# Attention's elementwise work moved from Pool to ACT and DVE, and k's halves copied by DVE instead of DMA

## The chip, the cores and the metric

The kernel runs on one core of a Trainium2 chip. The metric is the device time of one execution in microseconds. A core has five engines with queues of their own: PE (matrix products), DVE (vector work), ACT (activations and scaled copies), Pool (general work) and SP, which here only issues DMA transfers. DMA transfers run on 16 engines that the core shares among its queues.

## The reference

Three stages follow one another. The arrays are float32.

```python
# attention: B, H, S, D = 8, 8, 576, 64, causal in blocks of 64
scores = (1 / sqrt(D)) * q @ k.T, masked to block_i >= block_j
attn = softmax(scores);  x = (attn @ v) as [4608, 512]
# gated MoE without routing: w1, w2 [512, 1024], w3 [1024, 1024], w_out [1024, 512]
x = ((x @ w1) * (x @ w2)) @ w3 @ w_out
# routed experts: 8 experts, 576 tokens each, assigned greedily by sorted logits x @ w_gate
out[tokens of e] = relu(x[tokens of e] @ ew1[e]) @ ew2[e]
```

## The kernel before

**Split numbers.** To multiply float32 data on PE in f16, a tensor is scaled by a power of two and split into hi, its f16 rounding, and lo, the f16 rounding of what is left. A product is hi*hi + hi*lo + lo*hi. The power of two comes from a sum of squares: `ssq` on ACT (L115), `total` on PE (L453), `pow2` on DVE (L75 to L78).

**The steps of attention.** A step n (0 to 31) handles one pair of heads of one batch, and `step(n)` (L648) writes its work in order. `s_tiles` (L217) computes the scores of nine query blocks i = 0 to 8 in six tiles: S on PE (L226), the row maximum on DVE (L231, with L284 for row 8), exp on ACT (L265, L286, L287), the sum and its reciprocal on DVE (L289, L237, L238). `fin` (L241) then writes the hi and lo of the probabilities into `Pb`: hi of row blocks 4 to 7 on Pool (L250), of 8 on DVE (L254), of 0 to 3 on ACT (L252), and lo on DVE (L255). Row block i is (i+1) x 64 wide; `blocks` (L205) cuts it into a first piece of up to 384 columns and pieces of at most 128. `transP` (L306) sends `Pb` through two DMA transposes, and `pv` (L312) of the next step multiplies by v.

**Preparation for later steps.** Between the first tile and the others, step n loads q and k of step n+2 (`load_qk`), prepares q and k of step n+1 (`prep_qk`, L175) and the part of v it needs (`prep_v`, L147). `prep_qk` scales on Pool in place (L193), rounds to hi on ACT (L194), subtracts to lo on Pool (L195); step 0 alone does this on ACT and DVE (L189, L190). A DMA transpose on SP's queue (L197) then gives `T`: T[:, 0] has q with hi in partitions 0 to 63 and lo in 64 to 127, T[:, 1] has k likewise, and T[:, 2] is to have k's halves exchanged. Two transfers on SP's queue (L200) copy the halves crosswise. `qkT` has two buffers, `qk16` one. The second transfer of step 0 is `gate["d"]`: the loads of v of the first batch are issued behind it (L607).

**Weights.** Spread over the steps through `fills`, w1, w2 and w3 are decoded on DVE (`decode`, L429) and split by `scaled` (L443): Pool, ACT, Pool. `wo_split` (L494) does the split on ACT and DVE already. From step 5 on, `moe_unit` (L341) computes the first matmuls of the MoE in between (L356, L361, L363), four units a step.

**Order.** Each engine runs its instructions in the order in which a planner put them, from a model of their durations; SP issues its transfers in order too, and a transfer whose data are not there holds the queue. An instruction waits for those of other engines by semaphores. After attention comes the rest of the MoE, then the routing, then the experts; Pool works there too (L966, L1103, L1150), and the diff doesn't touch that.

## Time and profile before

| | |
|---|---|
| runs shown | 1695.24, 1699.73, 1700.19 us; median 1699.73 |
| profiled execution | 1691.84 us, its span 1690.1 us |
| mean granted clock of PE | 0.941 |
| busy share of the span | PE 84%, DVE 67%, ACT 51%, Pool 30% |
| DVE's busy time up to 880 us, by the four stretches 0, 40, 360 and 400 us on | 14.60 + 295.12 + 22.70 + 387.24 us |

The shares are means over stages that have different limits, so the profile is read by stretches: 0 to about 880 us is attention with the first MoE matmuls, to about 960 us the rest of those, to about 1300 us the routing beside the last product, and then the experts. A busy time of an engine counts the time in which at least one of its instructions runs; an instruction that stands inside for something else counts as busy too. "Idle before" is the time that an engine stood still ahead of an instruction, and the name behind the arrow is what ended it.

### The profile page before, as it was taken

Reading aid. Unit: us, or ns where it says so; the run is one execution under the profiler, and the core shown is the slowest. Engines: PE = TensorE matmul, PEld = TensorE weight load, DVE = VectorE, ACT = ScalarE, POOL = GpSimd, SP = SyncE. Lnnn points to the kernel's source line nnn. Section 1 sums busy time; section 2 is a strip of 40 time slices with the busy share of each in tenths; the row PEclk is TensorE's granted clock in tenths of the full one; section 3 lists DMA queues with packets and bytes.
Section 4 is the critical chain, followed back from the end, with each engine's and each line's share of the span. In section 5 each row is a group of like instructions: output and inputs, shape, how many; then the busy total and the mean of one; then the engine's idle time right before and its main releaser. Section 6 shows DMA issues by size and latency. Waiting matters only on the chain.

```text
span 1690.1 us, 32656 instructions
## 1 busy us (share of the span) xinstructions
PE 1414.7 (84%) x11561; PEld 944.3 (56%) x11561; DVE 1136.9 (67%) x3972; ACT 863.1 (51%) x2211; POOL 500.2 (30%) x629
## 2 busy tenths in 40 slices
PE   1547768878788988889999988888886999999997
PEld 0325545556455655556566666655655656666664
DVE  3999999767897988888632178898884324353420
ACT  4666667656676666666432224343431456573721
POOL 4555654334654545454311000000002321100101
PEclk9867989989899999999999999999997999999999
DMA  7697988987999999997997352432435765462200
GB/s 170 131 189 163 195 195 198 194 187 154 188 188 211 182 208 194 192 205 160 241 233 242 103 194 77 143 130 90 144 101 134 197 133 180 132 191 84 82 26 31
DMA packets 575476, 270.04 MB, mean 160 GB/s; under 512 B 467281, under 2 KB 544593, under 8 KB 575313
## 3 DMA queue, kind: packets, MB, share of 16 engines
q1 hardware_dynamic: 567872, 246.95, 62.9%
q0 software_dynamic: 5760, 18.90, 3.5%
q10 hardware_dynamic: 1680, 2.11, 0.4%
q8 instruction: 90, 1.47, 0.3%
q14 instruction: 74, 0.60, 0.1%
HBM read 131.57 MB, written 39.86 MB: 101 GB/s over the span
## 4 chain that ended last, share of the span: by engine, by line
PE 26%; DVE 20%; issue 14%; DMA 8%; ACT 4%; POOL 2%; SPq 2%; POOLq 0%; ACTq 0%; DVEq 0%
PE px L976 7%; PE ab L356 6%; PE pe L1128 4%; DVE P L255 3%; PE pe L1145 3%; DVE gl L993 2%; DVE junk L231 2%; DMA qkT<-qk 2%; DMA xg<-xr,idx 1%; POOL out_dram L1150 1%; PE lgp L397 1%; ACT gh L991 1%; DVE row L1006 1%; PE PV L552 1%; DVE ewb L1057 1%
## 5 line engine op out<-in xcount | busy, mean ns | idle before, releaser
L356 PE MATMUL ab<-xT,w2h 128*128 128x288 f16 x1536 | 229.7, 299 | 23.5 <-DVE g L363 22.9
L255 DVE SCALAR_TENSOR_TENSOR P<-E,rr,P 128x64 f16<-128x64 f32 (+3 forms) x480 | 239.4, 534 | 11.4 <-POOL P L250 7.9
L356 PE MATMUL ab<-xT,w1h 128*128 128x288 f16 x1536 | 232.0, 300 | 18.0 <-DVE xT L336 7.9
L1128 PE MATMUL pe<-xT,ewa 128*128 128x288 f16 (+2 forms) x1728 | 193.8, 276 | 11.2 <-DMA xT<-xg 10.3
L356 PEld LDWEIGHTS <-w2h 128*128 128x128 f16 x1536 | 150.2, 102 | 84.8 <-issue 40.7
L356 PEld LDWEIGHTS <-w1h 128*128 128x128 f16 x1536 | 150.6, 103 | 77.6 <-issue 33.2
L250 POOL TENSOR_SCALAR P<-E,rr 128x384 f16<-128x384 f32 (+3 forms) x224 | 117.7, 537 | 250.6 <-DVE rr L238 122.6
L265 ACT ACTIVATE E<-S,nb,cc 128x256 f32<-128x256 f32 (+7 forms) x256 | 149.2, 587 | 81.7 <-DVE junk L231 47.5
L1145 PE MATMUL pe<-ewb,h 128*128 128x512 f16 (+1 forms) x960 | 189.1, 379 | 1.1 <-DVE h L1131 1.1
L226 PE MATMUL S<-qkT 128*64 128x64 f16 (+7 forms) x1280 | 132.1, 323 | 63.4 <-DMA qkT<-qkT 21.1
L1128 PEld LDWEIGHTS <-ewa 128*128 128x128 f16 x1728 | 158.4, 100 | 45.4 <-issue 11.8
L1103 POOL DMA_INDIRECT xg<-xr,idx x36 | 34.8, 965 | 481.7 <-DVE idx L952 387.9
L231 DVE TENSOR_SCALAR_CACHE_REDUCE junk<-S,cc 128x512 f16<-128x512 f32 (+4 forms) x320 | 155.1, 508 | 16.8 <-PE S L226 16.6
L1145 PEld LDWEIGHTS <-h 128*128 128x128 f16 (+1 forms) x960 | 85.4, 101 | 100.4 <-issue 3.8
L1131 DVE SCALAR_TENSOR_TENSOR h<-pe,h 128x288 f16<-128x288 f32 (+2 forms) x144 | 57.6, 420 | 109.0 <-ACT h L1130 106.5
L226 PEld LDWEIGHTS <-qkT 128*64 128x64 f16 x1280 | 65.8, 119 | 110.8 <-issue 67.7
L329 PE MATMUL PV<-PT,v 128*64 128x256 f16 (+4 forms) x1536 | 105.0, 264 | 25.2 <-DMA PT<-P 20.4
L976 PE MATMUL px<-W34l,gh 128*128 128x512 f32 x288 | 122.7, 426 | 0.0
L976 PE MATMUL px<-W34h,gh 128*128 128x512 f32 x288 | 122.0, 424 | 0.0
L976 PE MATMUL px<-W34h,gl 128*128 128x512 f32 x288 | 121.7, 423 | 0.0
L363 DVE SCALAR_TENSOR_TENSOR g<-ab,vr,a_sb 128x288 f32<-128x288 f32 x124 | 63.1, 508 | 76.9 <-PE ab L356 39.9
L329 PEld LDWEIGHTS <-v 128*64 128x64 f16 (+1 forms) x1536 | 75.9, 113 | 61.1 <-issue 55.8
(283 smaller groups left out, 2539.5 us busy)
## 6 DMA issues: line engine op xcount, KB each, us to landing
g<-gd SPq DMA_DIRECT2D x36, 512.0 KB
gd<-g SPq DMA_DIRECT2D x124, 144.0 KB
g<-gd SPq DMA_DIRECT2D x15, 1152.0 KB
raw<-in_moe_w_dram SPq DMA_DIRECT2D x32, 512.0 KB
esa<-in_moe_w_dram SPq DMA_DIRECT2D x8, 2048.0 KB
esb<-in_moe_w_dram SPq DMA_DIRECT2D x8, 2048.0 KB
xr<-row SPq DMA_DIRECT2D x36, 256.5 KB
qkT<-qkT SPq DMA_DIRECT2D x64, 144.0 KB
```

What stands on the lines that cost most here:

```text
L226: nc.tensor.matmul(ps[hh * 64:hh * 64 + 64, o:o + N], T[:, 0, qc:qc + 64], T[:, z, kc:kc + N], start=z == 1, stop=z == 2)
L231: nc.vector.tensor_scalar(j[:, :N], ps[:, o:o + N], c[:, 1:2], None, op0=ALU.mult, op1=ALU.min, accum_out=dst)
L250: nc.gpsimd.tensor_scalar(hi, src, r, 1.0, op0=ALU.mult, op1=ALU.mult)
L255: nc.vector.scalar_tensor_tensor(lo, src, r, hi, op0=ALU.mult, op1=ALU.subtract)
L265: nc.scalar.activation(e[:, o:o + N], ps[:, o:o + N], AF.Exp, bias=nb[:, 0, x:x + 1], scale=c[:, 0:1], accum_out=nb[:, 1, x:x + 1])
L329: nc.tensor.matmul(ps[hh * 64:hh * 64 + 64, (lo - i0) * 64:(i1 - i0) * 64], vt[:kk, zv, hh, j, :], t[:kk, zp, ix:ix + i1 - lo, hh * 64:hh ...
L356: nc.tensor.matmul(p[:, :288], w[:, zw, cc, :], x[:, zx, cc, c0:c0 + 288], start=first, stop=cc == 3 and zw == 1)
L363: nc.vector.scalar_tensor_tensor(g, ps["w2"][:, :288], iv[b][:, 1, f:f + 1], a, op0=ALU.mult, op1=ALU.mult)
L976: nc.tensor.matmul(p, gh[a][:, f], W34[b][:, f], start=f == 0 and a + b == 0, stop=f == 7 and a == 1)
L1128: nc.tensor.matmul(p[:, :n], w1[:, a, cc, f * P:(f + 1) * P], t[:, 4 * b + cc, x], start=cc == 0 and a + b == 0, stop=cc == 3 and a == 1)
L1131: nc.vector.scalar_tensor_tensor(h[:, 1, f, x], p[:, :n], 0.0, h[:, 0, f, x], op0=ALU.max, op1=ALU.subtract)
L1145: nc.tensor.matmul(p[r0:r1], h[:, a, f, k_ * P + r0:k_ * P + r1], EW[e, "b"][0][:, b, f], start=f == 0 and a + b == 0, stop=f == 7 and a == 1)
```

## The change

A new function `split` writes hi on ACT with the scale and lo on DVE from the unscaled data and the scale. `prep_v`, `prep_qk`, `scaled` and `wo_split` use it, so that nothing elementwise is left on Pool in this stage. In `fin`, hi of row blocks 5, 7 and 8 is on DVE and of the others on ACT. The crosswise copies of k's halves are instructions of DVE, and `gate["d"]` is now the transpose.

```diff
--- before.py
+++ after.py
@@ -29,8 +29,7 @@
 R3 = 2
 LE = 37
 SW = 30
-POOL_HI = (4, 5, 6, 7)
-DVE_HI = (8,)
+DVE_HI = (5, 7, 8)
 TH = 5
 TB = 15
 TBX = 5
@@ -98,6 +97,10 @@
     ps_s = pa.enter_context(tc.tile_pool(name="ps_s", bufs=3, space=PSUM))
     ps_v = pa.enter_context(tc.tile_pool(name="ps_v", bufs=2, space=PSUM))
 
+    def split(hi, lo, x, s):
+        nc.scalar.activation(hi, x, AF.Copy, scale=s)
+        nc.vector.scalar_tensor_tensor(lo, x, s, hi, op0=ALU.mult, op1=ALU.subtract)
+
     gate = {}
     qk32, qkT, vst, vhl, xT, PT = {}, {}, {}, {}, {}, {}
     sc_c, iv, sv, ivs = {}, {}, {}, {}
@@ -152,9 +155,7 @@
         h = slice(2 * hp, 2 * hp + 2)
         for a, z in ((t[:, h, :4, :], lambda y: vt[:, y, :, :4, :]), (t[:64, h, 4, :], lambda y: vt[:64, y, :, 4, :])):
             np_ = a.shape[0]
-            nc.gpsimd.tensor_scalar(a, a, s[:np_], 1.0, op0=ALU.mult, op1=ALU.mult)
-            nc.scalar.activation(z(0), a, AF.Copy)
-            nc.gpsimd.tensor_tensor(out=z(1), in0=a, in1=z(0), op=ALU.subtract)
+            split(z(0), z(1), a, s[:np_])
         vhl[n] = vt
 
     def scale_x(b):
@@ -185,19 +186,12 @@
         sc_c[n] = c
         t16 = c2.tile([P, 2, 9, 2, D], F16, name="qk16", bufs=1)
         for z in range(2):
-            if n == 0:
-                nc.scalar.activation(t16[:, z, :, 0, :], t[:, z], AF.Copy, scale=s[:, z:z + 1])
-                nc.vector.scalar_tensor_tensor(t16[:, z, :, 1, :], t[:, z], s[:, z:z + 1], t16[:, z, :, 0, :],
-                                               op0=ALU.mult, op1=ALU.subtract)
-                continue
-            nc.gpsimd.tensor_scalar(t[:, z], t[:, z], s[:, z:z + 1], 1.0, op0=ALU.mult, op1=ALU.mult)
-            nc.scalar.activation(t16[:, z, :, 0, :], t[:, z], AF.Copy)
-            nc.gpsimd.tensor_tensor(out=t16[:, z, :, 1, :], in0=t[:, z], in1=t16[:, z, :, 0, :], op=ALU.subtract)
+            split(t16[:, z, :, 0, :], t16[:, z, :, 1, :], t[:, z], s[:, z:z + 1])
         T = c2.tile([P, 3, 9 * P], F16, name="qkT")
-        nc.sync.dma_start_transpose(out=T[:, :2].rearrange("p z (c r) -> p (z c) r", r=P),
-                                    in_=t16.rearrange("p z c h d -> p (z c h d)"))
+        d = nc.sync.dma_start_transpose(out=T[:, :2].rearrange("p z (c r) -> p (z c) r", r=P),
+                                        in_=t16.rearrange("p z c h d -> p (z c h d)"))
         for x in range(2):
-            d = nc.sync.dma_start(T[64 * (1 - x):64 * (2 - x), 2], T[64 * x:64 * x + 64, 1])
+            nc.vector.tensor_copy(T[64 * (1 - x):64 * (2 - x), 2], T[64 * x:64 * x + 64, 1])
         qkT[n] = T
         if n == 0:
             gate["d"] = d
@@ -246,12 +240,10 @@
                     src = e[:, k0:k0 + n_].rearrange("p (b c) -> p b c", c=P)
                 else:
                     hi, lo, src = pb[:, 0, idx, :n_], pb[:, 1, idx, :n_], e[:, k0:k0 + n_]
-                if i in POOL_HI:
-                    nc.gpsimd.tensor_scalar(hi, src, r, 1.0, op0=ALU.mult, op1=ALU.mult)
-                elif i not in DVE_HI:
+                if i in DVE_HI:
+                    nc.vector.tensor_scalar(hi, src, r, None, op0=ALU.mult)
+                else:
                     nc.scalar.activation(hi, src, AF.Copy, scale=r)
-                else:
-                    nc.vector.tensor_scalar(hi, src, r, None, op0=ALU.mult)
                 nc.vector.scalar_tensor_tensor(lo, src, r, hi, op0=ALU.mult, op1=ALU.subtract)
 
         def some(ps, lst):
@@ -442,9 +434,7 @@
 
     def scaled(w, m2, hi, lo, name):
         s, e = pow2(sm, m2, name)
-        nc.gpsimd.tensor_scalar(w, w, s, 1.0, op0=ALU.mult, op1=ALU.mult)
-        nc.scalar.activation(hi, w, AF.Copy)
-        nc.gpsimd.tensor_tensor(out=lo, in0=w, in1=hi, op=ALU.subtract)
+        split(hi, lo, w, s)
         return e
 
     def total(m):
@@ -500,8 +490,7 @@
         t = wo["t"] = stg.tile([P, 8, 2, 512], F16, name="wo16", bufs=1)
         for c in range(8):
             w = wo["w"][:, c]
-            nc.scalar.activation(t[:, c, 0], w, AF.Copy, scale=s)
-            nc.vector.scalar_tensor_tensor(t[:, c, 1], w, s, t[:, c, 0], op0=ALU.mult, op1=ALU.subtract)
+            split(t[:, c, 0], t[:, c, 1], w, s)
         wo["wg"], wo["eg"] = hilo(wo["g"], 4, "wgx")
 
     def wo_dot():
```

## Rows read from the trace of the kernel before

**Rows 1.** Busy us (instructions) of each engine by stretch, from the view of stretches
```profile
core 0: us, PE busy (x) PEld busy (x) DVE busy (x) ACT busy (x) POOL busy (x), PEclk, DMA share, GB/s
40.00:360.00 320.00, 221.37 (x1914) 148.84 (x1914) 295.12 (x995) 210.06 (x591) 170.15 (x218) 0.84 0.87 182
400.00:880.00 480.00, 418.10 (x3837) 272.39 (x3836) 387.24 (x1305) 286.75 (x794) 222.01 (x296) 0.95 0.94 198
880.00:960.00 80.00, 77.98 (x609) 52.35 (x609) 15.74 (x38) 21.55 (x41) 9.33 (x4) 0.98 0.65 203
```

**Rows 2.** The chain that ended last, 400 to 880 us, shares by line
```profile
by line: DVE P L255 11.5%; PE ab L356 10.8%; DVE junk L231 6.9%; issue 6.5%; DMA qkT<-qk 5.6%; PE PV L552 3.6%; PE PV L329 3.3%; DMA PT<-P 2.7%; DVE g L363 2.7%; DVE nb L289 2.5%; DVE rr L237 2.4%; PE S L226 1.9%; ACT E L286 1.8%; DVE P L25
```

**Rows 3.** DVE's groups by shape, 0 to 880 us (count | busy us, mean ns | idle before)
```profile
L255 DVE SCALAR_TENSOR_TENSOR P<-E,rr,P 128x384 f16<-128x384 f32 x128 | 91.1, 712 | 6.8 <-POOL P L250 6.7
L255 DVE SCALAR_TENSOR_TENSOR P<-E,rr,P 128x64 f16<-128x64 f32 x160 | 61.7, 396 | 1.8 <-ACT P L252 1.7
L255 DVE SCALAR_TENSOR_TENSOR P<-E,rr,P 128x128 f16<-128x128 f32 x128 | 58.7, 460 | 1.0 <-ACT P L252 0.8
L289 DVE TENSOR_TENSOR nb<-nb 128x1 f32<-128x1 f32 x32 | 22.3, 696 | 23.8 <-ACT E L287 23.8
```

**Rows 4.** The same groups from 840.5 to 850.4 us, and that stretch's engines
```profile
840.50:850.40 9.90, 9.90 (x70) 5.12 (x69) 7.76 (x33) 4.73 (x13) 0.00 (x0) 0.78 0.94 163
L255 DVE SCALAR_TENSOR_TENSOR P<-E,rr,P 128x384 f16<-128x384 f32 x2 | 1.2, 612 | 0.0
L255 DVE SCALAR_TENSOR_TENSOR P<-E,rr,P 128x64 f16<-128x64 f32 x3 | 0.8, 276 | 0.0
L255 DVE SCALAR_TENSOR_TENSOR P<-E,rr,P 128x128 f16<-128x128 f32 x1 | 0.3, 344 | 0.0
L289 DVE TENSOR_TENSOR nb<-nb 128x1 f32<-128x1 f32 x1 | 0.2, 159 | 0.9 <-ACT E L287 0.9
L254 DVE TENSOR_SCALAR P<-E,rr 128x128 f16<-128x128 f32 x1 | 0.3, 276 | 0.0
```

**Rows 5.** DVE's groups, 0 to 880 us, as in rows 3: prices of like work
```profile
L190 DVE SCALAR_TENSOR_TENSOR qk<-qk,qp,qk 128x576 f16<-128x576 f32 x2 | 1.5, 814 | 0.5 <-ACT qk L189 0.5
L504 DVE SCALAR_TENSOR_TENSOR wo<-wo,wop,wo 128x512 f16<-128x512 f32 x8 | 5.8, 762 | 0.0
L254 DVE TENSOR_SCALAR P<-E,rr 128x384 f16<-128x384 f32 x32 | 19.5, 608 | 0.4 <-DVE rr L238 0.3
L733 DVE TENSOR_TENSOR Tc<-dpf,iok 128x1152 f16<-128x1152 f16 x2 | 1.5, 745 | 0.0
```

**Rows 6.** A line's instructions (min/median/max ns), and two neighbours of DVE's timeline
```profile
L902 DVE TENSOR_SCALAR um<-upper x1: 168/168/168, 838.6 to 838.6; 128x128 f16<-128x128 f16 x1
...
585.95 0.16 DVE L238 RECIPROCAL rr<-rr 128x1 f32<-128x1 f32 x1
586.02 0.67 DVE L231 TENSOR_SCALAR_CACHE_REDUCE junk<-S,cc 128x448 f16<-128x448 f32 x1
```

**Rows 7.** ACT's groups by shape, 0 to 880 us
```profile
L252 ACT ACTIVATE P<-E,rr 128x256 f16<-128x256 f32 x32 | 16.1, 503 | 12.1 <-DVE rr L238 6.5 <-DVE rr L237 2.8 <-issue 2.1
L252 ACT ACTIVATE P<-E,rr 128x64 f16<-128x64 f32 x64 | 21.8, 340 | 3.4 <-DVE rr L238 3.3
```

**Rows 8.** Waits, 40 to 880 us, SP's own queue from 0 (total, times, longest us)
```profile
DVE P L255 <- POOL P L250: 7.9, 17, 0.8
PE S L226 <- DMA qkT<-qkT: 21.1, 10, 4.0
SPq L200 <- DMA qkT<-qk: 20.2, 24, 1.9
```

**Rows 9.** The timeline of the first 48 us (start us, duration us)
```profile
20.38 3.45 SPq L131 DMA_DIRECT2D v<-in_v_dram  x4
37.22 3.56 DVE L289 TENSOR_TENSOR nb<-nb 128x1 f32<-128x1 f32 x1 [1.38 <-ACT E L287]
```

**Rows 10.** DMA issues of the page, with KB of one
```profile
qkT<-qkT SPq DMA_DIRECT2D x64, 144.0 KB
```

## The prediction

> **What bounds the kernel now.** I read the stages first: a window table of busy time per engine [rows 1]. The change touches attention, which runs together with the first MoE matmuls from 0 to about 880 us. From 40 to 360 us DVE is busy 295.1 of 320 us (92%) and PE 221.4 (69%): there DVE sets the pace. From 400 to 880 us DVE is busy 387.2 of 480 us (81%) and PE 418.1 (87%), and neither fills the time alone. The DMA engines stand at 0.87 and 0.94. From 880 to 960 us PE is busy 78.0 of 80, and nothing the change edits runs in that stretch or behind it. Which work goes into which step is written out in advance, so what attention saves arrives later unchanged.
>
> The chain of work that ended last comes next [rows 2]. From 400 to 880 us its largest name is DVE's subtraction L255 with 11.5%, ahead of the main matmuls L356 with 10.8%, and the transposes of k and q have 5.6%. So DVE's time and the way of k into S are what the change can shorten or lengthen.
>
> Third, the instruction groups of DVE, which show that its busy time is not all work. L255 takes 712 ns for 384 columns, 396 for 64 and 460 for 128 over the stage, and the one-column L289 takes 696 ns [rows 3]. In a stretch of 9.9 us in which Pool does nothing, the same forms take 612, 276, 344 and 159 ns [rows 4]. The longest L289, 3.56 us for one column, stands at 37.22 us in the middle of Pool's work on v [rows 9]. I read the difference as DVE waiting inside its instructions for Pool.
>
> **Part 1, Pool's work goes away.** The gain on DVE is the two means' difference times the count: L255 with 384 columns 128 x 0.100 = 12.8 us, with 64 columns 160 x 0.120 = 19.2, with 128 columns 128 x 0.116 = 14.8, L289 32 x 0.537 = 17.2: 64.0 us [rows 3, 4]. Nine more groups treated the same way (L255 with 256 columns, L237, L284, L183, L434, L436, L437, L438, L254) give, by my estimate, 81 more. That makes 145 us of DVE's busy time in the stage, bounded by 64 below. The waits for Pool between instructions are small beside it: L255 stood 7.9 us for Pool's hi parts [rows 8]. I take -8 for that; the next thing late there is ACT, which now writes the hi of rows 4 and 6.
>
> **Part 2, what DVE takes over.** The price of each lo comes from DVE's own lines that do the same now:
> - q and k: 62 x 0.814 = 50.5 us [rows 5].
> - v: 32 with 512 columns at 0.762 [rows 5] and 32 with 128 at 0.344 [rows 4]: 35.4.
> - weights: 16 x 0.762, and 8 with 1024 columns, estimated at 1.30 (512 columns more at the 1.05 ns below): 22.6.
> - hi of rows 5 and 7: 64 x 0.608 [rows 5] and 32 x 0.276 [rows 4]: 47.7.
> - copies of the halves of k: 64 of 64 x 1152 f16. None is in the trace. The nearest row above is a two-input f16 instruction with just 1152 columns, 745 ns [rows 5]; the nearest below is a one-input f16 instruction with 128 columns, 168 ns [rows 6]. L255 costs 268 ns for 256 columns more, 1.05 ns each [rows 4]; 128 columns of f16 in 168 ns leave little over a one-column instruction's 159, so I take a quarter of that rate: 0.14 + 1152 x 0.26 = 0.44 us, 28.2 us in all (bounds 10.8 and 47.7).
>
> Together 184.4 us in 312 instructions. DVE begins an instruction some 0.09 us before the one ahead of it ends (585.95 + 0.16 against 586.02, [rows 6]); with 0.07 for each I take off 22 and get 163. DVE's net is 163 - 145 = +18 us.
>
> Where it falls matters more than the net. From 40 to 360 us, 12 of the 32 steps, DVE is full, and the net counts: 12/32 of 18, **+7**. From 400 to 880 us, 19 steps, what goes away lies mostly in the softmax line itself (L255, L289 and the small ones; I take two thirds of the 145 us, 3 us of every step), and what comes is mostly preparation of the next step, which can fill DVE's 93 idle us. DVE's five names in [rows 2] make 26% of the chain; with the names that the row leaves out I put its share at 0.4, an estimate. That is 57 x 0.4 = -23; of the 97 us added I let half fall into idle time, +97 x 0.5 x 0.4 = +19: **-4**.
>
> **Part 3, ACT.** It takes the hi of rows 4 and 6, two wide and two narrow ones a step: 32 x (0.503 + 0.340 + an estimated 0.6 + 0.340) = 57 us [rows 7]; what the scale adds to its other copies is small beside it. At 210 of 320 and 287 of 480 us [rows 1] it has room; what an exp may wait behind a hi I put at **+5** (0 to 20).
>
> **Part 4, the way of k.** Transpose, wait in SP's queue, two transfers, S becomes transpose, two copies on DVE, S. PE stood 21.1 us for those transfers, up to 4.0 at a time [rows 8]; two copies take 0.9 us, so I take **-14** (0 to -21). SP loses 64 issues and the wait in front of them, 20.2 us in 24 steps, behind which loads, the g stores and the next transposes were queued: **-4** (0 to -10). The wait moves to DVE. Behind the copies on DVE stand the maxima and reciprocals of the running step, and ACT's exps wait for those. SP stood at most 1.9 us for a transpose [rows 8], and DVE is more often late than SP: **+6** (0 to +20). The transfers were 64 x 144 KB = 9.4 MB [rows 10], some 47 us at the stage's 198 GB/s with the engines at 0.94: **-6** (0 to -26).
>
> **Part 5, the start.** The loads of v are tied behind the crosswise transfer of step 0; now they follow the transpose, and their issue moves from 20.38 to about 18 us. The 3.4 us that L289 stood at 37.22 goes [rows 9]. Together **-6** (0 to -8).
>
> **The sum:** -8 + 7 - 4 + 5 - 14 - 4 + 6 - 6 - 6 = **-24 us**. The profiled execution took 1691.8 us, so 1667.8 on its scale; the median of the runs is 1699.7, 7.9 above it, and on that scale the forecast is **1676**.
>
> A copy that crosses the partition halves could cost more than its length. In the trace neighbours on DVE overlap by 0.09 us [rows 6]. The Trainium skill (VectorE: DVE Perf Modes, Two Vector instructions with no wait between them) says that an instruction whose input or output starts in another quarter of the partitions than the previous ones starts only when all earlier ones have finished. By that rule both copies and the instruction behind them would lose the overlap, 3 x 32 x 0.09 = 9 us of DVE, and the sum would be -15. No row of the kernel before shows such a pair, and I keep the sum.
>
> **The rivals.**
> - **The whole wait was on the path.** If DVE's waiting for Pool lay on the late stage's chain in full and the added work goes into DVE's idle 93 us in full, the late term is -57 instead of -4: -77, 1623. For it: ACT and PE mostly wait for DVE. Against it: PE at 87% there leaves 62 us at most.
> - **Hidden.** The hops through Pool and the transfers had a whole step of 25 us to hide in, and DVE's net is paid: the -8, -14 and -4 of parts 1 and 4 are nothing, and +7 - 4 + 5 + 6 - 6 - 6 = +2 is left: 1702.
> - **DVE stands before the copies** (slower). The copy waits in DVE's in-order queue for a transpose which is late because the DMA engines are at 0.94. If it is placed too early by x us, DVE stands x in each of 32 steps. I have charged 6 us; the change loses when 32x is over 30, that is from x = 0.95 us on. At the 1.9 us that SP stood at most it is 61, net +31: 1731. For it: 24 of 32 transposes were not there when SP came. Against it: DVE is the busier queue.
> - **Pool is not the cause.** If DVE's long instructions have another cause, the 145 us stay, the late -23 and half of the start's gain go, and +54 comes early: -24 + 23 + 54 + 3 = +56, 1756. Against it: the stretch without Pool [rows 4].
>
> **How the numbers follow.** Forecast 0.42, whole wait on the path 0.22, hidden 0.15, DVE stands before the copies 0.16, other cause 0.05. A measurement tells a difference from none from about 0.3% on, 5 us. The forecast and the first rival are faster, plus a little of the hidden case: 0.66. Same is most of the hidden case and the forecast's edge, 0.13. Slower is the two last: 0.21. The range goes from 1630, which leaves the far half of the first rival out, to 1715, which cuts the two slow ones in the middle. The forecast's own range is 1655 to 1694.
>
> **What would show it.** Right: L289 near 160 ns and L255 with 384 columns near 612; DVE's busy time to 880 us within 20 us of before; copies near 0.44 us; ACT's busy time some 57 us up; no PE wait for the crosswise transfer; the first L289 before 37 us. Wrong: idle time of DVE ahead of the copies, released by the transposes, of more than 30 us; PE waiting for ACT's evictions more than before; copies at 0.75 us or more.

## The result, and the profile after

| | before | changed |
|---|---|---|
| median of 12 runs each, on the same chip | 1696.44 us | 1707.49 us |
| ratio, with its 95% interval | 1 | 1.0058 [1.0039, 1.0077] |
| profiled execution, its span | 1690.1 us | 1701.1 us |
| busy over the whole span: DVE, ACT, Pool | 1136.9, 863.1, 500.2 us | 1144.4, 916.4, 92.7 us |

The kernel became slower by 0.58%, some 10 us, where 24 us less were forecast. The time lies inside the range; the sign is wrong. In the two profiled executions, step 0 reaches the first cut of the stretches shown further down 4.0 us earlier, the next 12 steps take 10.7 us longer, the 19 after them 6.6, and all that follows takes 2.3 less. Below, 1% is taken as 17 us, since the kernel before takes 1697.

The view of stretches of the changed kernel answers to [rows 1], with the same columns: busy us (instructions) of each engine, granted clock of PE, DMA share, GB/s.

```profile
40.00:360.00 320.00, 224.97 (x1898) 149.22 (x1896) 284.19 (x1077) 221.99 (x612) 0.00 (x0) 0.85 0.80 167
400.00:880.00 480.00, 405.85 (x3766) 269.74 (x3766) 393.85 (x1486) 315.63 (x870) 5.99 (x13) 0.95 0.87 182
880.00:960.00 80.00, 76.84 (x665) 51.94 (x663) 14.97 (x34) 21.12 (x40) 9.39 (x4) 1.00 0.76 233
```

Pool is all but empty and the DMA engines have room (0.80 and 0.87 where it was 0.87 and 0.94). DVE is busy 11 us less from 40 to 360 us and 7 more from 400 to 880; ACT is busy 12 and 29 us more, with the most room of the three. PE's granted clock is what it was. No engine is near its limit that was not so before, and the kernel is slower all the same.

Second, DVE's groups by shape, 0 to 960 us, against [rows 3, 5] (count | busy us, mean ns | idle before). L247 is the subtraction that was L255, L281 the one-column instruction that was L289, L102 the lo of the new `split`, L194 the copies, L244 hi.

```profile
L247 DVE SCALAR_TENSOR_TENSOR P<-E,rr,P 128x384 f16<-128x384 f32 x128 | 77.5, 609 | 4.9 <-ACT P L246 4.8
L247 DVE SCALAR_TENSOR_TENSOR P<-E,rr,P 128x64 f16<-128x64 f32 x160 | 42.5, 276 | 0.0
L281 DVE TENSOR_TENSOR nb<-nb 128x1 f32<-128x1 f32 x32 | 4.9, 153 | 4.1 <-ACT E L279 4.0
L244 DVE TENSOR_SCALAR P<-E,rr 128x384 f16<-128x384 f32 x96 | 58.1, 605 | 0.2
L102 DVE SCALAR_TENSOR_TENSOR qk<-qk,qp,qk 128x576 f16<-128x576 f32 x64 | 50.4, 810 | 9.6 <-ACT qk L101 9.0 <-DMA qk<-in_q_dram 0.5
L194 DVE COPY qkT<-qkT 64x1152 f16<-64x1152 f16 x64 | 29.1, 455 | 32.7 <-DMA qkT<-qk 31.9
```

The waiting inside instructions is gone from the groups shown: 712 became 609 ns, 396 became 276, 696 became 153, which are the values of the stretch without Pool [rows 4]. The new work costs what was put down for it: 810 ns where 814 was taken, 605 for 608, 455 for 440.

Third, the waits from 40 to 880 us (total, times, longest us), against [rows 8]. The first two lines are of the kernel before, the others of the changed one.

```profile
PE PV L329 <- DMA PT<-P: 20.4, 17, 3.1
PE ab L356 <- ACT a_sb L361: 1.6, 5, 0.5
PE ab L348 <- ACT a_sb L353: 14.7, 16, 2.7
PE PV L321 <- DMA PT<-P: 70.0, 38, 5.4
DVE qkT L194 <- DMA qkT<-qk: 31.9, 21, 4.4
```

PE's wait for the crosswise transfer is no longer in the list. Two others stand there instead: DVE stands 31.9 us for the transposes ahead of its copies, and PE stands 70.0 us for the transposed probabilities, where it stood 20.4. These were the first two suspects. PE's wait for ACT's copies of the MoE products (`a_sb`) has grown too, from 1.6 to 14.7 us.

Last, the start, against [rows 9]. The loads of v are issued at 16.09 us instead of 20.38, and the first L281 stands at 32.50 us with 0.16 us, where L289 was at 37.22 with 3.56.

```profile
16.09 3.61 SPq L134 DMA_DIRECT2D v<-in_v_dram  x4
32.50 0.16 DVE L281 TENSOR_TENSOR nb<-nb 128x1 f32<-128x1 f32 x1 [1.12 <-ACT E L279]
```

### The profile page after: what moved, and what is told of

The parts are those of the page before. It is cut to its first block, busy times and chain, and to the rows that moved or that the text cites. A ratio compares the mean times of both kernels' runs of the same rounds, so it can differ in the third digit from the quotient of the medians.

```text
span 1701.1 us, 32219 instructions
## 1 busy us (share of the span) xinstructions
PE 1416.2 (83%) x11561; PEld 947.3 (56%) x11561; DVE 1144.4 (67%) x4284; ACT 916.4 (54%) x2339; POOL 92.7 (5%) x101
## 4 chain that ended last, share of the span: by engine, by line
PE 30%; DVE 22%; DMA 22%; issue 15%; ACT 6%; SPq 3%; POOL 1%; POOLq 0%; ACTq 0%; DVEq 0%
PE ab L348 8%; DMA PT<-P 7%; PE px L965 7%; DMA qkT<-qk 5%; PE pe L1117 4%; PE pe L1134 3%; DVE P L247 3%; DVE junk L225 2%; DVE gl L982 2%; PE PV L321 2%; DMA raw<-in_moe_w_dram 2%; DVE P L244 1%; SPq L126 1%; DMA xg<-xr,idx 1%; DMA qk<-in_k_dram 1%
## 5 line engine op out<-in xcount | busy, mean ns | idle before, releaser
L348 PE MATMUL ab<-xT,w2h 128*128 128x288 f16 x1536 | 229.5, 298 | 18.2 <-DVE g L355 8.4
L348 PE MATMUL ab<-xT,w1h 128*128 128x288 f16 x1536 | 228.8, 297 | 18.4 <-ACT a_sb L353 9.8
L247 DVE SCALAR_TENSOR_TENSOR P<-E,rr,P 128x64 f16<-128x64 f32 (+3 forms) x480 | 178.1, 409 | 5.7 <-ACT P L246 5.6
L321 PE MATMUL PV<-PT,v 128*64 128x256 f16 (+4 forms) x1536 | 113.2, 283 | 71.6 <-DMA PT<-P 71.5
L225 DVE TENSOR_SCALAR_CACHE_REDUCE junk<-S,cc 128x512 f16<-128x512 f32 (+4 forms) x320 | 155.8, 509 | 15.5 <-PE S L220 14.7
L220 PE MATMUL S<-qkT 128*64 128x512 f16 (+7 forms) x1280 | 128.2, 323 | 38.6 <-ACT E L257 19.2
L321 PEld LDWEIGHTS <-v 128*64 128x64 f16 (+1 forms) x1536 | 83.6, 121 | 109.2 <-issue 96.5
L246 ACT ACTIVATE P<-E,rr 128x64 f16<-128x64 f32 (+3 forms) x288 | 103.0, 418 | 35.5 <-DVE rr L232 25.5
L980 ACT ACTIVATE gh<-g 128x1024 fp32r<-128x1024 f32 x36 | 38.1, 1060 | 144.0 <-PE px L965 139.1
L353 ACT ACTIVATE a_sb<-ab,vr 128x288 f32<-128x288 f32 x128 | 63.3, 495 | 91.7 <-PE ab L348 88.4
```

The lines of the kernel that those rows point to most:

```text
L220: nc.tensor.matmul(ps[hh * 64:hh * 64 + 64, o:o + N], T[:, 0, qc:qc + 64], T[:, z, kc:kc + N], start=z == 1, stop=z == 2)
L225: nc.vector.tensor_scalar(j[:, :N], ps[:, o:o + N], c[:, 1:2], None, op0=ALU.mult, op1=ALU.min, accum_out=dst)
L246: nc.scalar.activation(hi, src, AF.Copy, scale=r)
L247: nc.vector.scalar_tensor_tensor(lo, src, r, hi, op0=ALU.mult, op1=ALU.subtract)
L321: nc.tensor.matmul(ps[hh * 64:hh * 64 + 64, (lo - i0) * 64:(i1 - i0) * 64], vt[:kk, zv, hh, j, :], t[:kk, zp, ix:ix + i1 - lo, hh * 64:hh ...
L348: nc.tensor.matmul(p[:, :288], w[:, zw, cc, :], x[:, zx, cc, c0:c0 + 288], start=first, stop=cc == 3 and zw == 1)
```

## The experiments

Theories went by letters. **A**: DVE stands before the copies, the slow rival of the prediction. **B**: PE stands for the transposed probabilities because the pieces of `Pb` come late. **C**: the hi parts of rows 4 and 6 on ACT cost the time. **D**: those of rows 5 and 7 on DVE cost it. When D stood, three ways remained: **D1**, the place (the softmax line, between a step's sum and its transposes); **D2**, the data's way (hi and lo of a row now stand in one queue); **D3**, DVE's time as such, wherever it is spent. All diffs are against the changed kernel unless another is named. Ratios are to the kernel before, measured beside each; busy times are those of the whole span, so that the same work is in each.

| kernel | ratio [95%] | DVE, ACT, Pool busy us |
|---|---|---|
| changed | 1.0058 [1.0039, 1.0077] | 1144.4, 916.4, 92.7 |
| e1_transfers_back | 1.0066 [1.0044, 1.0088] | 1119.2, 914.5, 93.2 |
| e2_copies_alone | 1.0033 [1.0016, 1.0051] | 1171.3, 863.5, 497.6 |
| e3_hi_on_pool | 0.9935 [0.9910, 0.9960] | 1122.2, 873.9, 227.9 |
| e4_copies_on_pool | 1.0023 [0.9996, 1.0050] | 1145.6, 913.6, 173.9 |
| e5_hi46_on_pool | 1.0067 [1.0049, 1.0084] | 1149.2, 876.5, 188.0 |
| e6_hi57_on_pool | 0.9886 [0.9860, 0.9913] | 1113.6, 914.6, 151.3 |
| e7_splits_alone | 0.9960 [0.9941, 0.9978] | 1094.4, 871.7, 226.3 |
| e8_act_doubles_hi46 | 0.9983 [0.9968, 0.9998] | 1117.9, 915.3, 231.1 |
| e9_dve_doubles_hi57 | 0.9995 [0.9974, 1.0017] | 1147.7, 914.7, 153.0 |
| e11_hi_4to7_on_act | 0.9997 [0.9975, 1.0019] | 1110.1, 955.6, 93.3 |
| e12_hi57_and_copies_on_pool | 0.9885 [0.9854, 0.9917] | 1120.5, 913.8, 237.1 |
| e13_dve_doubles_in_prep | 1.0043 [1.0016, 1.0069] | 1146.9, 917.0, 152.0 |
| o1_hi57_left_out | 0.9925 [0.9908, 0.9942] | 1107.1, 913.5, 92.9 |
| o2_changed_null_edit | 1.0038 [1.0019, 1.0056] | 1147.0, 915.6, 93.0 |
| o3_hi57_pool_null_prep | 0.9908 [0.9884, 0.9932] | 1115.5, 913.9, 152.3 |
| o4_hi57_pool_null_tile | 0.9921 [0.9897, 0.9945] | 1114.4, 914.2, 151.9 |
| p0_pool_tiny | 1.0070 [1.0044, 1.0097] | 1145.1, 915.9, 205.5 |
| p2_pool_load | 1.0479 [1.0452, 1.0506] | 1280.2, 917.8, 393.8 |

### Which part of the change it is

**The copies undone.**

```diff
-            nc.vector.tensor_copy(T[64 * (1 - x):64 * (2 - x), 2], T[64 * x:64 * x + 64, 1])
+            d = nc.sync.dma_start(T[64 * (1 - x):64 * (2 - x), 2], T[64 * x:64 * x + 64, 1])
```

> The changed kernel with the two crosswise transfers on SP's queue put back in place of DVE's copies; the splits and the hi parts stay on ACT and DVE. Theory A (DVE stands before the copies: 31.9 us of idle time in the changed kernel's trace, released by the transposes): the loss goes and the rest of the change shows its gain, some 10 to 25 us faster than the kernel before, ratio 0.985 to 0.995. Theory B (the new order of the hi parts on ACT and DVE makes the probabilities come later against PE's order, PE stands 70.0 us before PV for DMA PT<-P against 20.4): no better than the changed kernel, ratio 1.003 to 1.010.

1.0066. DVE loses 25 us of work and the time does not move; PE's wait for the crosswise transfer is back. The restored line sets `d` again, so that the loads of v stand behind the transfer of step 0 as in the kernel before; this holds for e7 too.

```profile
PE S L220 <- DMA qkT<-qkT: 16.3, 11, 3.8
PE PV L321 <- DMA PT<-P: 64.4, 39, 4.5
```

The copies are not the cause, but neither did they bring what was expected of them.

**The copies alone**, in the kernel before: the line above the other way round, with `d` taken from the transpose.

> The kernel before with the copies on DVE (and the loads of v behind the transpose) alone; Pool keeps all its work. Theory A: DVE stands some 30 us before the copies and the copies also wait for Pool inside, so 10 to 30 us slower than before, ratio 1.006 to 1.018. Theory B: the copies cost only their 29 us of DVE against 21 us of PE's wait, ratio 0.998 to 1.005.

1.0033: slower by 6 us, although the loads of v start earlier. With DVE still waiting for Pool, the 34 us more on DVE cost more than the transfers did.

**The hi parts of rows 4 to 7 back on Pool.**

```diff
-DVE_HI = (5, 7, 8)
+POOL_HI = (4, 5, 6, 7)
+DVE_HI = (8,)
...
-                if i in DVE_HI:
+                if i in POOL_HI:
+                    nc.gpsimd.tensor_scalar(hi, src, r, 1.0, op0=ALU.mult, op1=ALU.mult)
+                elif i in DVE_HI:
```

> The changed kernel with the hi parts of row blocks 4 to 7 back on Pool; splits and copies as changed. Theory A: still slow, ratio 1.003 to 1.012, with DVE's idle time before the copies near 30 us. Theory B: PE's wait before PV returns to some 20 to 30 us, and the time comes to that of before or below, ratio 0.99 to 1.0.

0.9935: the loss sits in the four hi parts. The waits of this kernel, 40 to 880 us:

```profile
PE PV L324 <- DMA PT<-P: 69.8, 39, 4.5
DVE qkT L195 <- DMA qkT<-qk: 32.8, 20, 4.5
```

Both suspicious waits are as long as in the changed kernel, in a kernel that is 1.2% faster. A and B fall as explanations of the loss: the waits are there, but nothing that the changed kernel lost hangs on them.

**The copies on Pool.**

```diff
-            nc.vector.tensor_copy(T[64 * (1 - x):64 * (2 - x), 2], T[64 * x:64 * x + 64, 1])
+            nc.gpsimd.tensor_copy(T[64 * (1 - x):64 * (2 - x), 2], T[64 * x:64 * x + 64, 1])
```

> The changed kernel with the copies of k's halves on Pool, which does nothing else then, so the wait for the transposes holds an idle queue; two transfers are still saved. Theory A: 29 us of DVE's work and 32 us of its idle time go, 15 to 30 us faster than the changed kernel, ratio to before 0.985 to 0.997. Theory B: PE's wait before PV stays near 70 us, ratio 1.002 to 1.008.

1.0023, 6 us under the changed kernel, no more than the order alone can move (below). DVE is freed of 64 copies and is as busy as before (1145.6 against 1144.4): Pool's 81 us more come back to it as waiting.

**Rows 4 and 6 on Pool, 5 and 7 on DVE**: `POOL_HI = (4, 6)` in the diff of e3, `DVE_HI` as changed.

> The changed kernel with the hi parts of row blocks 4 and 6 on Pool; 5, 7 and 8 stay on DVE. ACT loses the 57 us that the change gave it, DVE keeps its 48. Theory C (ACT's added hi parts are what costs): close to the run with all four on Pool, ratio to before 0.990 to 0.997. Theory D (DVE's added hi parts cost): close to the changed kernel, 1.002 to 1.008.

1.0067. Taking ACT's share back gives nothing, so C falls. Against e3, where all four are on Pool, this kernel has only the hi of rows 5 and 7 moved to DVE, and it is 22 us slower.

**Rows 5 and 7 on Pool, 4 and 6 on ACT**: `POOL_HI = (5, 7)`, `DVE_HI = (8,)`.

> The changed kernel with the hi parts of row blocks 5 and 7 on Pool and of 4 and 6 on ACT as changed. DVE loses 48 us, ACT keeps its 57. Theory C: still slow, 1.002 to 1.008. Theory D: 0.990 to 0.997.

0.9886, median 1673.26 us: faster than both kernels, 29 us under the changed one, and below the range expected for D. D holds: what loses is hi of rows 5 and 7 on DVE. The wait of A is 40.8 us in this kernel:

```profile
DVE qkT L195 <- DMA qkT<-qk: 40.8, 23, 4.2
```

**The splits alone**, in the kernel before: `split` in `prep_v`, `prep_qk`, `scaled` and `wo_split`, hi on Pool, the transfers as before, and with them `gate["d"]` on the second transfer.

> The kernel before with only the splits of v, k, q and the weights moved to ACT and DVE; hi parts of the probabilities on Pool and the crosswise transfers as before. If the copies cost what they cost alone (ratio 1.0033) whatever stands beside them, this is 0.33% below the run with hi on Pool and copies on DVE (0.9935): 0.990. If the copies cost nothing once Pool's splits are gone, as in the run with the transfers put back, 0.992 to 0.995.

0.9960, above both expected values (0.990, and 0.992 to 0.995). DVE is 42 us less busy than in the kernel before, and the gain is only 7 us.

In steps from before to changed: splits -7, copies with the earlier loads of v -4 (e3), rows 4 and 6 to ACT -8 (e6), rows 5 and 7 to DVE +29. The sizes depend on the order of the steps: by way of e5, rows 5 and 7 to DVE are +22 and rows 4 and 6 to ACT -2.

### Whose time it is

**ACT's time.** In the kernel of e3, ACT writes the hi of rows 4 and 6 a second time, into a tile that nobody reads.

```diff
+                if i in (4, 6):
+                    dj = sm.tile([P, 384], F16, name="dj", bufs=2)
...
+                    nc.scalar.activation(dv, src, AF.Copy, scale=r)
```

> The run with all four hi parts on Pool, and ACT also writes those of row blocks 4 and 6 into a tile that nobody reads: 128 more instructions, some 57 us of ACT, in the same place of the program. Theory C as time of ACT: the loss comes back without any change of the data's way, 1.000 to 1.006. Theory C as the way of the data (lo and the transposes wait for ACT's queue), or Theory D: no change, 0.991 to 0.997.

0.9983, between the two expected ranges: 0.48% over e3, 8 us for 41 us of ACT.

**All four on ACT**: `DVE_HI = (8,)`.

> The changed kernel with the hi parts of row blocks 4 to 7 all on ACT, 8 alone on DVE; Pool stays empty in the stage. DVE loses 48 us, ACT has some 50 more than in the changed kernel. D1, D2, D3: DVE's loss goes, 0.986 to 0.995, if ACT has the room; if ACT is full by then (some 650 of 960 us busy) the gain is eaten, 0.997 to 1.004.

0.9997, 19 us over e6, with DVE at 1110 us and ACT at 956. These hi parts are not free on ACT either: against o1 (below), where nobody writes them, it is 12 us for 42 us of ACT.

**DVE's time, same place.** In the kernel of e6, Pool keeps the hi of rows 5 and 7, and DVE writes them a second time, unread.

```diff
+                if i in (5, 7):
+                    dj = sm.tile([P, 3, 2 * P], F16, name="dj", bufs=2)
...
+                    nc.vector.tensor_scalar(dv, src, r, None, op0=ALU.mult)
```

> The run with the hi parts of row blocks 5 and 7 on Pool (0.9886), and DVE also writes them, in the same place, into a tile that nobody reads, with the same strides: 96 more instructions, some 48 us of DVE; the data's way stays over Pool. D1 (DVE's time in the softmax line is what costs) and D3 (DVE's time anywhere costs): the loss comes back, 0.998 to 1.006. D2 (the way of the data, lo and the transposes behind DVE's hi): no change, 0.986 to 0.992.

0.9995, 18 us over e6 for 34 us more on DVE. Nobody waits for these results, so D2 falls as the main cause: time alone does 18 of the 29 us.

**DVE's time, another place.** The same 96 instructions, unread, in `prep_qk`, where the next step is prepared.

```diff
+        for w in (3, 3, 1):
+            dj = sm.tile([P, 3, 2 * P], F16, name="dj", bufs=2)
...
+            nc.vector.tensor_scalar(dv, src, s[:, 0:1], None, op0=ALU.mult)
```

> The same base with three instructions of DVE of the same sizes and strides in each step (96 in all, some 48 us), but behind the split of q and k of the next step instead of in the softmax line, into a tile that nobody reads. D1: little, 0.988 to 0.995. D3: 0.998 to 1.006. D2: no change, 0.986 to 0.992.

1.0043, 27 us over e6 for 33 us. D1 falls: preparation is not a cheaper place. D3 is left, as far as two places show it.

**The work left out.** In the changed kernel the hi of rows 5 and 7 is not written: it stays zero, and lo holds the whole probability in f16.

```diff
-                if i in DVE_HI:
+                if i in (5, 7):
+                    pass
+                elif i in DVE_HI:
```

> The changed kernel with the hi parts of row blocks 5 and 7 not written at all (they stay zero, and lo then holds the whole f16 value): DVE is without their 48 us, and Pool and ACT have nothing for them. If DVE's time is what costs: 0.982 to 0.992, at or below the run with these hi parts on Pool (0.9886). If the order of the instructions is what costs and each edit draws a new one: anywhere from 0.985 to 1.007.

0.9925: 23 us less than changed for 37 us less on DVE. It was expected at or below e6 and is 7 us above it.

**The copies on Pool, in the kernel of e6**: the line of e4 in it.

> The run with the hi parts of 5 and 7 on Pool (0.9886), and the copies of k's halves on Pool too. DVE no longer stands before the transposes (40.8 us there) and loses 29 us of work. If that wait cost time, 0.978 to 0.985; in the changed kernel the same edit gave 0.35%, which would be 0.985; if the wait is slack, 0.987 to 0.990.

0.9885, as e6. Even where DVE stands 40.8 us before the copies, freeing its queue of them gives nothing. The copies on Pool make DVE wait inside its instructions again (it is busy 6.9 us more although 25 us of copies left it), so this alone does not price the wait at nothing; with e1 and e3, nothing speaks for A any more.

### What the order alone moves

A planner orders all instructions anew after each edit. Three kernels ask what that is worth, each with 32 one-column memsets on DVE that nobody reads.

```diff
+        nl = sm.tile([P, 1], F32, name="nl", bufs=2)
+        nc.vector.memset(nl, 0.0)
```

In `prep_qk` of the changed kernel:

> The changed kernel with one memset of one column on DVE in each step's preparation of q and k, 32 in all, 2 us together, into a tile that nobody reads: work that can't matter, but the planner draws a new order. If DVE's time is what costs: as the changed kernel, 1.003 to 1.009. If the order that the planner happens to draw is worth as much as the edits tested so far: off that by 0.5% or more, 0.990 to 1.001.

In `prep_qk` of e6:

> The run with the hi parts of 5 and 7 on Pool (0.9886) with the same memset in the preparation of q and k. DVE's time: 0.985 to 0.992. The order: off by 0.5% or more, 0.994 to 1.005.

Ahead of the first tile in `s_tiles` of e6:

> The same base with the memset in front of each step's first tile of scores instead. DVE's time: 0.985 to 0.992. The order: off by 0.5% or more, 0.994 to 1.005.

1.0038, 0.9908 and 0.9921, against 1.0058 and 0.9886: -3, +4 and +6 us. The third is a hair over its expected range for DVE's time. Three draws do not bound what an order can do; differences of that size between two of these kernels are put down to nothing.

### Waiting for Pool, given back

The changed kernel gets Pool work that nobody reads: four one-input and four two-input instructions of 576 columns a step, in `prep_qk`. The second kernel has the same instructions with one column each, so that the two have one order of instructions: in the traces DVE, ACT and SP run the same sequence.

```diff
+    cst = const.tile([P, 576], F32, name="cst")
+    nc.gpsimd.memset(cst, 1.0)
...
+        for z in range(4):
+            dy = sm.tile([P, 576], F16, name="dy", bufs=1)
+            nc.gpsimd.tensor_scalar(dy, cst, s[:, z % 2:z % 2 + 1], 1.0, op0=ALU.mult, op1=ALU.mult)
+            nc.gpsimd.tensor_tensor(out=dy, in0=cst, in1=cst, op=ALU.subtract)
```

> The changed kernel with Pool loaded again by work that nobody reads: four one-input and four two-input instructions of 128 x 576 in each step, some 260 us of Pool (the kernel before had 416 up to 840 us). DVE's instructions should again wait for Pool inside themselves, some 80 to 110 us in all by the share of the kernel before (154 us of excess for its Pool). If such a wait costs as much as work of DVE does (0.45 to 0.9 us for each us by the hi parts), 40 to 90 us more than the next run; if it is cheap, as the small gain of the splits alone says (7 us for 145), under 20 us more.

> The same kernel with all those Pool instructions cut to one column. The instructions of DVE, PE, ACT and SP stand in the same order as in the run before, so the difference is Pool's load alone, without a new order. By itself as the changed kernel with a null edit: 1.000 to 1.010.

1.0479 against 1.0070, 69 us. DVE's groups, 0 to 960 us, with the short Pool work and then with the long:

```profile
L253 DVE SCALAR_TENSOR_TENSOR P<-E,rr,P 128x64 f16<-128x64 f32 x160 | 42.5, 276 | 0.0
L104 DVE SCALAR_TENSOR_TENSOR qk<-qk,qp,qk 128x576 f16<-128x576 f32 x64 | 50.3, 808 | 8.3 <-ACT qk L103 8.2
L282 DVE TENSOR_TENSOR nb<-nb 128x1 f32<-128x1 f32 x32 | 4.8, 151 | 0.1
```

```profile
L253 DVE SCALAR_TENSOR_TENSOR P<-E,rr,P 128x64 f16<-128x64 f32 x160 | 68.5, 438 | 0.0
L104 DVE SCALAR_TENSOR_TENSOR qk<-qk,qp,qk 128x576 f16<-128x576 f32 x64 | 73.8, 1174 | 2.7 <-ACT qk L103 2.7
L282 DVE TENSOR_TENSOR nb<-nb 128x1 f32<-128x1 f32 x32 | 13.4, 417 | 0.1
```

DVE's instructions are the same in both, and the long work of Pool makes them longer, one column too. So the rival that Pool is not the cause falls from both sides: the waiting goes with Pool's work and comes back with it. DVE is busy 135 us more (1280.2 against 1145.1), over the 80 to 110 expected, and the kernel pays 69: 0.51 us for each us of waiting.

## Why the sign was wrong

**The sizes were right.** The removed waiting was put at 145 us and the net on DVE at +18; DVE's busy time over the span rose by 7.5. The copy was put at 0.44 us and took 0.455, the lo of q and k at 0.814 and took 0.810; ACT rose by 53 us (57 expected); the one-column sum of step 0 (L289, now L281) came 4.7 us earlier (6 expected at the start); the crosswise wait went. Every mark that the prediction named for "right" is met, and so are two named for "wrong". One is the 31.9 us of DVE ahead of the copies, which e1, e3 and e6 clear. The other is PE's longer wait for ACT's copies of the MoE products, 14.7 us for 1.6; it is 14.9 in e6, which is 29 us faster, so the loss does not hang on it. The marks tested what things cost DVE; none tested what DVE's time costs the kernel.

**The step that failed is the price of DVE's time**, the last paragraph of part 2. It took 163 us added and 145 removed, and in the first stretch counted the two alike, as a net: "From 40 to 360 us, 12 of the 32 steps, DVE is full, and the net counts". The view of stretches, cut at the one-column maximum of row 8 of step 0, of step 12 and of step 31, shows otherwise. DVE's busy time is the third of the engine numbers. Of each kernel, the first line has the 12 steps and the second the 19 after them.

Before:

```profile
35.00:340.30 305.30, 211.28 (x1820) 142.27 (x1818) 280.34 (x941) 198.24 (x563) 164.79 (x210) 0.85 0.87 182
340.30:841.70 501.40, 429.45 (x3948) 283.52 (x3946) 410.14 (x1375) 305.09 (x837) 237.66 (x318) 0.95 0.93 192
```

Changed, and o2, which is changed with a null edit:

```profile
31.00:347.00 316.00, 221.51 (x1853) 146.16 (x1853) 279.37 (x1062) 219.72 (x612) 0.00 (x0) 0.86 0.78 167
347.00:855.00 508.00, 424.17 (x3916) 284.99 (x3915) 413.38 (x1551) 331.98 (x905) 5.99 (x13) 0.93 0.86 177
31.20:344.60 313.40, 221.99 (x1856) 147.38 (x1855) 279.25 (x1062) 219.44 (x612) 0.00 (x0) 0.82 0.79 168
344.60:846.10 501.50, 425.59 (x3913) 284.47 (x3912) 414.39 (x1551) 331.77 (x905) 5.98 (x13) 0.93 0.87 180
```

e6 (rows 5 and 7 on Pool), and o3 and o4, which are e6 with null edits:

```profile
31.20:330.20 299.00, 214.91 (x1845) 144.68 (x1846) 267.51 (x1030) 218.53 (x610) 23.26 (x36) 0.87 0.82 174
330.20:827.40 497.20, 424.23 (x3935) 283.28 (x3932) 397.02 (x1493) 333.31 (x911) 40.09 (x70) 0.95 0.88 183
30.90:335.30 304.40, 218.02 (x1843) 146.81 (x1842) 267.78 (x1029) 218.28 (x610) 23.42 (x36) 0.86 0.82 171
335.30:833.30 498.00, 426.14 (x3936) 285.31 (x3936) 397.52 (x1494) 332.90 (x910) 40.14 (x70) 0.94 0.87 183
30.90:334.10 303.20, 216.28 (x1843) 145.38 (x1842) 267.46 (x1029) 217.71 (x610) 22.81 (x36) 0.84 0.82 172
334.10:829.90 495.80, 424.35 (x3936) 283.26 (x3936) 396.93 (x1493) 333.53 (x910) 40.46 (x70) 0.94 0.88 183
```

e9 and e13 (e6 with doubles on DVE, in the softmax line and in preparation):

```profile
31.30:345.20 313.90, 214.04 (x1826) 141.89 (x1826) 280.33 (x1062) 219.44 (x611) 23.43 (x36) 0.86 0.79 168
345.20:840.40 495.20, 422.75 (x3919) 282.81 (x3921) 415.13 (x1543) 331.63 (x906) 41.39 (x70) 0.94 0.87 176
28.70:346.10 317.40, 214.32 (x1849) 144.69 (x1846) 282.10 (x1067) 220.97 (x616) 24.55 (x36) 0.82 0.78 167
346.10:853.00 506.90, 430.18 (x3925) 286.28 (x3924) 416.79 (x1554) 334.00 (x909) 38.83 (x70) 0.93 0.85 177
```

o1 (rows 5 and 7 left out):

```profile
30.50:330.40 299.90, 213.14 (x1838) 143.25 (x1837) 264.05 (x1031) 219.93 (x612) 0.00 (x0) 0.85 0.84 177
330.40:823.90 493.50, 423.42 (x3928) 283.21 (x3929) 392.69 (x1488) 329.23 (x904) 5.98 (x13) 0.94 0.87 182
```

The short Pool work (p0):

```profile
30.90:346.60 315.70, 218.75 (x1856) 145.35 (x1855) 279.16 (x1062) 219.93 (x612) 47.84 (x96) 0.80 0.78 167
346.60:851.70 505.10, 421.52 (x3913) 282.62 (x3912) 413.92 (x1551) 331.47 (x905) 64.13 (x157) 0.94 0.87 178
```

The long Pool work (p2):

```profile
33.90:380.40 346.50, 225.63 (x1856) 147.46 (x1855) 328.32 (x1062) 221.30 (x612) 112.25 (x93) 0.81 0.71 153
380.40:919.40 539.00, 426.51 (x3911) 286.80 (x3912) 491.59 (x1551) 331.93 (x905) 175.34 (x161) 0.93 0.80 167
```

The same steps are in each first line, so the lengths compare directly. Before to changed, DVE has 1.0 us less to do (280.3 to 279.4), and the twelve steps take 10.7 us longer (305.3 to 316.0): its idle time went from 25.0 to 36.6. A busy share of 92% did not mean that nothing but busy time counts. The pairs give the prices in the twelve steps, as us of length for each us of DVE's busy time:

- work: o1 to changed, 16.1 us for 15.3 (1.05); e6 to e9, 14.9 for 12.8 (1.16); e6 to e13, 18.4 for 14.6 (1.26); e6 to changed, where Pool loses the same parts, 17.0 for 11.9 (1.43). Part of this is e6's own order: with the null edits its twelve steps take 304.4 and 303.2 us instead of 299.0, while those of changed take 313.4 (o2) and 315.7 (p0) instead of 316.0. Against the means of the three (302.2 and 315.0 us), the four prices are 0.99, 0.92, 1.05 and 1.10, so about 1.
- waiting inside instructions: 30.8 us for 49.2 (0.63), from one pair with one order. DVE's idle time falls from 36.5 to 18.2 there: a part of such waiting takes the place of time in which DVE would have stood for another engine's result anyway. That the same part comes back as idle time when the waiting goes fits before and changed (25.0 to 36.6).

The removal itself can be read from e7, from which no price was taken:

```profile
33.70:344.50 310.80, 225.98 (x1865) 150.36 (x1862) 263.54 (x1012) 204.85 (x566) 56.09 (x84) 0.84 0.87 182
344.50:833.80 489.30, 422.27 (x3914) 280.24 (x3915) 384.47 (x1452) 307.19 (x834) 79.52 (x146) 0.95 0.94 195
```

Against the kernel before, its DVE is busy 16.8 us less in the twelve steps, and they take 5.5 us longer; in the 19 after, it is busy 25.7 less and they take 12.1 less. The splits added some 85 us of work in all (an estimate, below), and with DVE 42 us less busy they removed some 127 of waiting; 12 and 19 of 32 steps have their shares of both. With work at 1.0 to 1.1, the waiting removed early had a price of 0.55 to 0.62; later, with work at 0.35 to 0.43, of 0.39 to 0.45. Both are near the prices of the waiting given back.

In the 19 steps after, work costs 0.70, -0.11, 0.49 and 0.66 us in the same pairs, 0.43 in the mean (0.35 with the null edits), and waiting 33.9 us for 77.7 (0.44). There the two are close, though the pairs for work differ widely. The prediction had 0.4 for the two thirds of the waiting that it put into the softmax line, 0.27 for all of it, and, since "half" of the added work was to "fall into idle time", 0.2 for what it added. On balance nothing fell into idle time: over the 19 steps DVE's idle time was 91.3 us before and is 94.6 after. DVE stands there for other engines' results; the view of groups of the changed kernel, 347 to 855 us, has half of it ahead of two lines, the MoE products' and the copies'.

```profile
L355 DVE SCALAR_TENSOR_TENSOR g<-ab,vr,a_sb 128x288 f32<-128x288 f32 x73 | 37.1, 509 | 25.7 <-PE ab L348 10.6 <-issue 9.3 <-ACT a_sb L353 2.4
L194 DVE COPY qkT<-qkT 64x1152 f16<-64x1152 f16 x38 | 17.3, 455 | 24.3 <-DMA qkT<-qk 23.9
```

**The sum again with these prices.** In busy time the added work is about 150 us: 37 for rows 5 and 7 (o1), 25 for the copies (e1), and for the lo parts some 0.8 of their 106 us, so 85, as with rows 5 and 7. With +7.5 net, 142 were removed. First stretch: 150 x 12/32 = 56 at 1.1, near the prices of the single edits, is +62, and 142 x 12/32 = 53 at 0.63 is -34: +28 instead of +7. Later: 89 at 0.43 is +38, and 84 at 0.44 is -37: +1 instead of -4. The forecast of -24 becomes about +2. With the prices that take the null edits in, 1.0 early and 0.35 later, it becomes about -11. So this step accounts for 13 to 26 of the 34 us between the forecast and the result, +10 with an interval from 7 to 13. By itself it does not settle the sign: these prices are of single executions, and the order alone moved 3 to 6 us.

**Parts 4 and 5** were put at -18 and -6, without the copies' time on DVE. The runs have the two together, since the loads of v move with the copies, and with that time they gave -1 (e1 to changed), -4 (e7 to e3) and +6 (e2). DVE's 25 us at the prices above are some +16, so the rest came to -10 to -20 where -24 was written, and the copies eat most of it up. That is 4 to 14 us more of the miss. How it falls on the two stretches is open: e7 to e3 gave -7.5 us in the twelve steps and +11.6 in the 19, e1 to changed +0.5 and +8.1.

**Parts 1 and 3** cannot be split from the runs: rows 4 and 6 from Pool to ACT gave -8 (e3 to e6) or -2 (e5 to changed), where -8 for Pool's hops and +5 for ACT were written for all rows. ACT's 57 us were taken as nearly free; e8 puts 41 us of ACT at 8 us.

**The rivals.** The slow one, DVE before the copies, named a wait that came, 31.9 us, and a wrong price for it: undoing the copies gives nothing back. "Hidden", with 1702, was nearest to the time and for another reason. "The whole wait was on the path" counted in the other direction from what the runs show. That the time lies inside the range is luck: its upper end was set by the two slow rivals, and neither is what made the kernel slower.

**What stays open.** Why the doubles of e9 cost nothing in the last 19 steps, where the other pairs show 0.5 to 0.7; why the doubles in preparation cost 27 us and those in the softmax line 18; and why e6 gains 29 over the changed kernel where leaving the same work out gains 23. The last two are near what the order moves; the first is about twice that.

## What to carry to other kernels

A busy share, even of 92%, is not a price. Waiting inside an engine's instructions is partly slack that comes back as idle time when it goes (here it costs about 0.6 us each where DVE is 92% busy), while work put in its place costs about in full there (0.9 to 1.1); a trade of one for the other at equal busy time lost here. A small double of the work in question, unread, tells the price before the whole change is written. And of such a change, each part is to be timed alone: three of these four parts gain together 19 us (e6, 0.9886), and the fourth, which only made "nothing on Pool" complete, lost 29.

## What the runs showed of the hardware

**Pool's instructions weigh differently on DVE.** Per us of Pool's busy time, DVE was busy 0.45 us more with the long unread work (changed to p2: 301.1 us on Pool, 135.8 on DVE), about 0.37 with the copies (e6 to e12: 85.8 on Pool; DVE up by 6.9 though 25 of copies left it), 0.11 with the hi parts of rows 5 and 7 (o1 to e6: 58.4 and 6.5) and 0.05 with those of rows 4 and 6 (changed to e5: 95.3 and 4.8). With the short unread work it was next to nothing (changed to p0: 112.8 and 0.7). So the hi parts were the cheapest of these to leave on Pool. What in the instructions decides it was not tried.

**One column on Pool is not small.** In the kernel with the short Pool work, 0 to 960 us:

```profile
L194 POOL TENSOR_SCALAR dy<-cst,qp 128x1 f16<-128x1 f32 x128 | 65.6, 513 | 690.2 <-DVE qp L79 551.1 <-DVE qp L78 79.2 <-DVE wp L76 29.6
L195 POOL TENSOR_TENSOR dy<-cst 128x1 f16<-128x1 f32 x128 | 45.6, 356 | 10.7
```

513 and 356 ns for one column, where DVE takes about 150.

**A copy across the partition halves does not overlap with its neighbours.** DVE's timeline of the changed kernel:

```profile
430.86 0.93 DVE L194 COPY qkT<-qkT 64x1152 f16<-64x1152 f16 x2 [4.37 <-DMA qkT<-qk]
431.81 0.17 DVE L231 TENSOR_SCALAR rr<-nb 128x2 f32<-128x2 f32 x1
431.89 0.87 DVE L247 SCALAR_TENSOR_TENSOR P<-E,rr,P 128x384 f16<-128x384 f32 x2
```

The two copies take 0.93 us from 430.86 and the next instruction begins at 431.81, after them; that one still has 0.09 us to go when its successor begins at 431.89. So it is in all 32 steps of this trace: no copy begins before the instruction ahead of it has ended, and none is overlapped by the one behind it, with 13 to 14 ns between the two copies, while 3520 of the other 4187 neighbours on DVE overlap. The pairs agree with what the prediction took from the Trainium skill (VectorE: DVE Perf Modes, Two Vector instructions with no wait between them). What the lost overlap costs in time was not measured by itself.
